# Two interleaved layers of sliding-window attention and gated linear units: the transposes moved off the DMA queue

## The chip, the cores and the metric

The kernel runs on one core of a Trainium2 chip. The metric is device time in microseconds (us) of the whole launch; lower is better. The time before is a median of three runs. One more execution was taken with the hardware profiler, and all rows shown come from that one.

## The reference

Two kinds of layer, A and B, alternate twice over x of 2048 tokens and 512 features in bf16:

```
x = x + A(layernorm(x));  x = x + B(layernorm(x))      # and both once more
A: qkv = x @ wqkv;  32 heads of 16;  scores = q k^T / 4
   masked to 0 <= query - key < 256;  p = softmax(scores);  (p v) @ wo
B: (sigmoid(x @ w_gate) * (x @ w_up)) @ w_down          # 512 -> 1792 -> 512
```

The weights are the same in both rounds. The layer norm has no learned scale or shift.

## The kernel before

**Tiles and stages.** x stays on chip as 16 tiles of 128 tokens by 512 features (`xsb`). Each of the two rounds (L = 0, 1) does the same for every tile t:

- *Norm* (`layer_norm`, L629): mean and variance on VectorE (L649, L651), the inverse root on GpSimd (L662, L663), the normed tile `xn` on VectorE (L681). This happens twice per tile and round, ahead of the attention (key "p") and ahead of the GLU (key "g"), so 64 times. TensorE contracts over partitions, so `xn` must be turned into `xnT`. Ten tiles are turned by TensorE: four transposes of 128 by 128 into a PSUM bank (L704) and one copy to SBUF on ScalarE or VectorE (L738, L740). They are the first eight of the first attention and the GLU tiles 0 and 1 of the first round (`alone`, from OPT g1 and `turn`). The other 54 go in pairs through 27 DMA transposes on the SP queue (L728).
- *Projections*: q and k feature-major in groups of four tiles (L780, L811), v token-major (L847), each copied out of PSUM by ScalarE or VectorE. k is split in two masked halves (L826). V carries a column of ones per head, so that the values' matmul also yields the softmax's sum; two shifted copies of it are made by plain DMAs (L1388).
- *Scores and values*: a tile's scores are worked off in five visits (two for the last tile), 154 in all. A visit fills four PSUM banks (`Sps`; L1106, L1117, L1127), ScalarE takes the exponential (L1159), VectorE multiplies the masks in (L1037). Then `values` (L1161, matmul L1186) makes the outputs of 16 heads in one bank: four heads side by side in a column block, each head on 32 partitions (16 outputs, the sum, padding).
- *Attention output* (`after_values`, L1192): the bank is copied out to `OTs` (L738 or L740), a DMA transpose turns it token-major into `Oq` (L1205), VectorE takes the reciprocal of the sums (L1240) and multiplies (L1241) into `On`, and a second DMA transpose turns that into `OnT` (L1213), which the output projection reads (L970). L976 adds the result to x. For the first two tiles of round 0 both turns are made by TensorE instead (`turn_by_pe`, L1253; the norm reads PSUM).
- *GLU* (`glu_units`): gate and up matmuls (L875) on 1, 2 or 4 tiles at once, so 128, 256 or 512 columns; tanh on ScalarE (L893), product on VectorE (L901); `down_units` (L939), and L948 adds to x. The list GLU says which tiles go together.

**Order.** Nothing is ordered by the hardware alone: `Plan` is a small planner that runs when the kernel is built. It keeps a clock, one queue per engine with a priority per kind of task, and assumed costs in ns; each engine's instruction stream is what it picks. `pick` chooses TensorE's next step: a visit of scores no earlier than `pace` after the last one, the values when their masks are done, else a dense unit by rank. Dense units and values share four PSUM banks; a unit's bank is free when its copy is done. DMAs carry an assumed issue cost and slack. The priorities, slacks, ranks and paces stand in SEGMENTS, a table that may change them at every fifth visit. `keep_warm` (L1370) issues idle matmuls before the first weights land. Rings limit how far work runs ahead: 2 `xn` (pairs), 3 `xnT`, 1 `OTs`, 1 `Oq`, 1 `On`, 2 `OnT`.

Of the kernel before, what the change touches and what calls it, by code (L numbers as in the profile page):

```python
# [9 lines left out]
ALU = mybir.AluOpType  # L10
BF16 = mybir.dt.bfloat16
F32 = mybir.dt.float32
P = 128
# [43 lines left out]
def pool_ns(n):  # L57
# [5 lines left out]
GLU = [[[1, 1, 1, 1, 2, 2], [1, 1, 1, 1, 2, 2], [1, 1, 2, 2, 2], [1, 1, 1, 1, 1, 1, 1, 1], [2, 2, 2, 2], [1, 1, 2, 1, 1, 2], [2, 2, 4]], [[4, 4, 4, 2, 2], [4, 4, 4, 2, 2], [4, 4, 2, 2, 4]]]  # L63
# [6 lines left out]
ARRIVE = dict(x0=3280, x1=4280, x2=5600, k=8560, q=10000, v=10900)  # L70
# [3 lines left out]
RATE = ((10900, 40.0), (1e9, 345.0))  # L74
# [3 lines left out]
LINE_NS = 3550  # L78
# [3 lines left out]
OPT = dict(gu='SP', g1=1, bk=3, bq=2, wide=0, r0=2, g0=5, g2=0, x0=1, eps=1, hold=1, own=1, ck=0, cq=2, turn=2,  # L82
    split=0, mo=0, at=3, r1=1, near=1)
RANK = dict(x3=31008.59915082838, wd=1355.5443193096523)


class Late(dict):


    def __missing__(self, name):  # L90
        return {"vv": self["v"], "tp": 0, "tp_g": 2}[name] if name in ("vv", "tp", "tp_g") else self[name[:-1]]


SEGMENTS = {
    0: (False, dict(st_x0=16.387, ap_x0=6.225, xt_x0=7.482, st_x1=3.545, ap_x1=7.915, xt_x1=12.783, st_x=12.637,
        ap_x=12.681, xt_x=-4.829, st_p=-0.616, ap_p=7.606, xt_p=5.184, st_g=-0.445, ap_g=2.621, xt_g=-2.868,
        st_g0=3.679, ap_g0=-17.463, xt_g0=-4.767, tp=8.093, tp_g=6.212, q=-2.808, q0=10.418, q1=-21.607, k=-11.975,
        k0=12.49, k1=0.894, s=-4.824, s0=2.968, s1=4.16, v=-0.758, v0=18.344, v1=21.96, vv=-1.006, exp=-7.486,
        exp0=-1.374, m0=3.414, m00=5.808, e0=-7.871, e00=2.35, e1=1.881, e10=8.977, m2=1.191, m20=5.467, th=14.916,
        mu=-10.778, dn=-19.706, add=-0.599, add0=7.919, out=-15.994, mv=30.614, mv0=7.196, oq=-9.099, oq0=-8.293,  # L100
        no=9.304, no0=-3.84, on=10.221, on0=-11.559, vc=9.867, vc0=-2.298), dict(xt=3835, oq=509, on=2499, vc=2407),
        dict(tp=-26.503, o=-3.164, lead=15.979, far=73.841, v=2.438, g=58.124, d=37.228, feed=44.486,
        x3=31008.59915082838, wd=1355.5443193096523, go=147.94192547482436), 1500.53),
    5: (False, {}, {}, {}, 1500.53),
    10: (False, {}, {}, {}, 1500.53),
    15: (False, {}, {}, {}, 1500.53),
    16: (False, {}, {}, {}, 1690.96),
    20: (False, {}, {}, {}, 1690.96),
    25: (False, {}, {}, {}, 1690.96),
    26: (True, dict(st_p=1.672, ap_p=36.822, xt_p=-2.918, st_x=-11.841, ap_x=0.6, xt_x=14.582, st_g=-13.947,  # L110
        ap_g=-7.573, xt_g=7.949, q=-14.515, k=21.982, s=1.709, v=-1.564, exp=-39.767, m0=2.485, e0=7.8, e1=8.391,
        m2=14.841, th=1.045, mu=-20.576, dn=-2.4, add=-13.535, out=27.454, mv=35.926, oq=-4.313, no=8.505, on=12.109,
        vc=-17.889), dict(xt=240, oq=3128, on=2754, vc=10020), dict(tp=36.947, o=-40.166, lead=9.199, far=17.491,
        v=-2.507, g=13.193, d=13.247, feed=-46.58, go=607.5028023985727), 2727.3),
    30: (False, dict(ap_x=1.293, dn=-2.072), dict(oq=2609), dict(feed=-47.788), 2681.58),
    35: (False, dict(st_p=0.51, ap_g=-7.3, mu=-24.39), dict(oq=2664, on=2941), dict(o=-39.26, lead=12.63, go=494),
        2681.58),
    40: (False, dict(st_p=1.672, ap_g=-7.573, mu=-20.576), dict(xt=779, oq=2609, on=2754), dict(o=-40.166,
        lead=9.199, go=607.5028023985727), 2620.7),
    45: (False, dict(st_p=0.82), dict(xt=240), dict(g=8.75, go=213), 1879.3),  # L120
    50: (False, dict(st_p=1.672), {}, dict(g=13.193, go=607.5028023985727), 2681.58),
    55: (False, {}, dict(xt=86), dict(lead=13.76), 2574.1),
    60: (False, {}, dict(xt=240), dict(lead=9.199), 2681.58),
    65: (False, {}, {}, {}, 2681.58),
    70: (False, {}, {}, {}, 2764.0),
    75: (False, {}, {}, {}, 2681.58),
    80: (False, {}, {}, {}, 2717.8),
    85: (False, dict(k=22.27, e0=8.47), {}, dict(far=18.98, v=-3.32, g=13.07), 2632.8),
    90: (False, dict(q=-15.93, k=21.982, e0=7.8, e1=11.21, add=-11.69), dict(on=2458), dict(lead=9.39, far=17.491,
        v=-2.507, g=14.8), 2717.8),  # L130
    95: (False, dict(q=-14.515, e1=8.391, add=-13.535), dict(on=2754), dict(lead=9.199, g=13.193), 2717.8),
    100: (False, {}, {}, {}, 2717.8),
    105: (False, {}, {}, {}, 2717.8),
    110: (False, {}, {}, {}, 2717.8),
    115: (False, {}, {}, dict(go=877), 2868.0),
    120: (False, {}, {}, dict(go=607.5028023985727), 2717.8),
    125: (False, {}, {}, {}, 2717.8),
    130: (False, {}, {}, {}, 2717.8),
    135: (False, {}, dict(oq=2597), dict(lead=8.49, far=16.64), 2717.8),
    140: (False, {}, dict(oq=2609), dict(lead=9.199, far=17.491), 2717.8),  # L140
    145: (False, {}, {}, {}, 2717.8),
    150: (False, {}, {}, {}, 2717.8),
}


def segments():

    out, now = {}, [Late(), {}, {}, 0]
    for slot, (new, prio, slack, rank, pace) in SEGMENTS.items():
        now = [Late(prio) if new else Late({**now[0], **prio}), {**now[1], **slack}, {**now[2], **rank}, pace]  # L150
        out[slot] = now
    return out
# [263 lines left out]
class Net:  # L416


    def __init__(self, ctx, tc, A_x, wqkv, wo, w_gate, w_up, w_down, out):
# [44 lines left out]
        ring("xn", 2, [P, 2, D])  # L464
# [4 lines left out]
        ring("On", 1, [P, 8, 4, 16])  # L469
# [159 lines left out]
    def layer_norm(self, key, t, deps):  # L629

        nc, pl = self.nc, self.pl
        alone = key[:2] == ("p", 0) and t < NBG * (1 + OPT["g1"]) or key[0] == "g" and self.by_pe(key[1], t)
        done = self.xn_ready[key, t]
        if alone:
            box, tiles = {"i": 0}, [t]
        else:
            box = self.pairs.setdefault((key, t // 2), {"i": t % 2, "ready": []})
            tiles = [t // 2 * 2, t // 2 * 2 + 1]
        mine = 0 if alone else t % 2
# [5 lines left out]
        def stats(e):  # L645
            if "st" not in box:
                box["st"] = self.take("st")
            st = box["st"][0][:, mine]
            nc.vector.bn_stats(out=st[:, 0:6], in_=self.xsb[:, t, :])  # L649
            if not first:  # L650
                nc.vector.bn_aggr(out=st[:, 6:8], in_=st[:, 0:6])  # L651

        def moments(e):
            st = box["st"][0][:, mine]
            nc.vector.bn_aggr(out=st[:, 6:8], in_=st[:, 0:6])
            nc.vector.tensor_scalar(out=st[:, 9:10], in0=st[:, 7:8], scalar1=1e-5, scalar2=None, op0=ALU.add)

        def root(e):
            st = box["st"][0]
            n = len(tiles)  # L660
            if not first:
                nc.gpsimd.tensor_scalar(out=st[:, 0:n, 9:10], in0=st[:, 0:n, 7:8], scalar1=1e-5, scalar2=None, op0=ALU.add)  # L662
            nc.gpsimd.tensor_tensor(out=st[:, 0:n, 8:9], in0=st[:, 0:n, 9:10], in1=self.nhalf[:, 0:n].rearrange("p (n x) -> p n x", x=1),  # L663
                                    op=ALU.pow)
# [10 lines left out]
        def apply(e):  # L675
            box["xn"] = b = self.take("xn")
            if key not in self.xnT:
                self.xnT[key] = self.take("xnT")
            for k, tt in enumerate(tiles):
                st = box["st"][0][:, k]  # L680
                nc.vector.tensor_scalar(out=b[0][:, k, :], in0=self.xsb[:, tt, :], scalar1=st[:, 6:7], scalar2=st[:, 8:9],  # L681
                                        op0=ALU.subtract, op1=ALU.mult)
# [6 lines left out]
        if not alone:  # L689
            box["ready"].append(a.done)  # L690
            if len(box["ready"]) < 2:
                return
        b = pl.task({"POOL": 800 - 230 * first}, root, box.get("ready", [a.done]), self.prio["st_" + kind])
        self.roots[key + (t,)] = b.done
        c = pl.task({"DVE": 60 + 346 * len(tiles)}, apply, [b.done], self.prio["ap_" + kind], can, port=True)
# [3 lines left out]
        i = tiles[0] % NBG  # L699
        if alone:  # L700
            def steps(bank):
                pt = self.tp_view(bank)
                xn = box["xn"][0][:, 0]
                return [(57, lambda c=c: nc.tensor.transpose(pt[:, c, :], xn[:, c * P:(c + 1) * P], self.ident[:]))  # L704
                        for c in range(KT)]

            def evac(u):
                pt = self.tp_view(u.bank)
                if key == ("p", 0, 0) and t < OPT["split"]:
                    half, both = KT // 2, Event()  # L710
# [9 lines left out]
            def ready():  # L720
                u = Unit(("tp", t), steps, [], False, evac)
                if key == ("p", 0, 0) and OPT["own"]:
                    u.own = BANKS + t
# [873 lines left out]
```

## Time and profile before

| what | us |
|---|---|
| median of three runs | 540.66 (540.53 to 541.17) |
| the profiled execution | 540.86 |
| its span, first to last instruction | 539.1 |
| busy: TensorE / VectorE / ScalarE / GpSimd | 524.0 / 417.1 / 384.8 / 43.6 |
| exponentials (L1159), 154 | 283.0 |
| GLU matmuls (L875), 1456 recorded | 256.5 |

In the profile's rows PE is TensorE's matmuls, PEld its weight loads (they overlap), DVE VectorE, ACT ScalarE, POOL GpSimd, and SPq the queue from which SyncE issues DMAs. L with a number is a line of the kernel. A group's row gives line, engine, operation, out<-in, shape and count; then busy us and mean ns of one; then the idle time of the engine just before them. A row of the timeline gives start and duration in us. A matmul's duration contains its way through the array, so several that follow each other overlap; their distance in time is what they cost. The granted TensorE clock was full in all 40 slices. Some matmul records are missing from a trace.

The 87 DMA transposes appear in the list of DMA issues with these median times from issue to landing: Oq<-OTs x30 3.3 us, OnT<-On x30 2.5 us, xnT<-xn x27 3.6 us.

### The profile page before, as it was taken

The page shows a single profiled execution, that of the slowest core. Times are in us where ns is not written, and L with a number is a line of the kernel's source. Part 1 is how long each engine was busy: PE and PEld are TensorE (multiplying, and loading weights), DVE is VectorE, ACT ScalarE, POOL GpSimd, SP SyncE. Part 2 cuts the span into 40 slices and gives each one's busy share as a digit, 9 for nine tenths or more (in the row PEclk, how much of TensorE's full clock was granted, in tenths as well). Part 3 has the DMA queues.
Part 4 walks back from the last instruction along what each step waited for, and adds up shares of the span by engine and source line. Part 5 has one row for each costly group of instructions (what it writes and reads, how often), then busy time and mean ns, then how long its engine had stood idle before and what let it go on. Part 6 is the DMA issues. An engine that isn't in the chain of part 4 may idle for free.

```text
span 539.1 us, 21310 instructions
## 1 busy us (share of the span) xinstructions
PE 524.0 (97%) x9606; PEld 293.1 (54%) x9674; DVE 417.1 (77%) x841; ACT 384.8 (71%) x384; POOL 43.6 (8%) x99
## 2 busy tenths in 40 slices
PE   8999999999999999999999999999999999999997
PEld 8446845758657544544444445444444454445873
DVE  6999989898798897779896989789787774442442
ACT  4999988979889797789688887688877751230330
POOL 4401100000001010000110100100000000000000
PEclk9999999999999999999999999999999999999999
DMA  8851533234223326225235323332143234101001
GB/s 259 320 149 52 82 82 52 53 71 74 39 56 42 72 41 93 50 56 72 47 51 72 52 54 45 68 61 62 33 80 52 51 43 75 34 1 39 2 11 39
DMA packets 95083, 36.23 MB, mean 67 GB/s; under 512 B 78352, under 2 KB 93968, under 8 KB 94992
## 3 DMA queue, kind: packets, MB, share of 16 engines
q1 hardware_dynamic: 93872, 33.82, 31.9%
q8 instruction: 75, 1.23, 1.0%
q10 hardware_dynamic: 1120, 1.05, 0.7%
q14 instruction: 16, 0.13, 0.1%
HBM read 9.70 MB, written 2.10 MB: 22 GB/s over the span
## 4 chain that ended last, share of the span: by engine, by line
PE 90%; ACT 4%; DVE 2%; issue 2%; DMA 1%; DVEq 0%
PE bank L875 36%; PE bank L939 18%; PE bank L1186 9%; PE Sps L1106 7%; PE bank L970 5%; PE bank L811 5%; PE bank L780 4%; PE bank L847 4%; PE Sps L1117 2%; ACT PTring L1159 2%; ACT edge L1159 1%; DMA xnT<-xn 1%; DMA xsb<-in_A_x_dram 0%; ACT qT L738 0%; DVE st L649 0%
## 5 line engine op out<-in xcount | busy, mean ns | idle before, releaser
L1159 ACT ACTIVATE PTring<-Sps 128x2048 bf16<-128x2048 f32 (+1 forms) x122 | 226.3, 1855 | 44.5 <-PE Sps L1106 41.0
L875 PE MATMUL bank<-xnT,wu 128*128 128x512 bf16 (+2 forms) x728 | 128.7, 297 | 0.5 <-issue 0.5
L875 PE MATMUL bank<-xnT,wg 128*128 128x512 bf16 (+2 forms) x728 | 127.8, 298 | 0.2 <-issue 0.2
L893 ACT ACTIVATE hT<-bank 128x256 bf16<-128x256 f32 (+1 forms) x154 | 71.5, 483 | 68.1 <-PE bank L875 67.5
L901 DVE SCALAR_TENSOR_TENSOR hT<-hT,bank 128x256 bf16<-128x256 bf16 (+1 forms) x154 | 80.6, 537 | 50.9 <-ACT hT L893 26.3
L939 PE MATMUL bank<-wd,hT 128*128 128x512 bf16 (+2 forms) x429 | 101.8, 372 | 3.2 <-issue 2.4
L875 PEld LDWEIGHTS <-wg 128*128 128x128 bf16 x728 | 61.2, 98 | 37.4 <-issue 2.7
L875 PEld LDWEIGHTS <-wu 128*128 128x128 bf16 x728 | 61.8, 98 | 35.3 <-issue 2.6
L939 PEld LDWEIGHTS <-hT 128*128 128x128 bf16 x462 | 42.5, 98 | 47.0 <-issue 1.9
L1159 ACT ACTIVATE edge<-Sps 128x2048 bf16<-128x2048 f32 (+1 forms) x32 | 56.7, 1773 | 13.4 <-PE Sps L1117 13.1
L1186 PE MATMUL bank<-PTring,Vaug 128*32 128x64 bf16 (+1 forms) x2880 | 51.8, 203 | 0.7 <-issue 0.7
L1186 PEld LDWEIGHTS <-Vaug 128*32 128x32 bf16 x2880 | 43.9, 97 | 12.3 <-issue 10.6
L1037 DVE TENSOR_TENSOR PTring<-PTring,mask 128x1024 bf16<-128x1024 bf16 x64 | 43.6, 683 | 7.9 <-ACT PTring L1159 7.7
L1106 PE MATMUL Sps<-qT,kTp 32*128 32x256 bf16 (+3 forms) x1216 | 47.4, 248 | 0.9 <-ACT edge L1159 0.4
L740 DVE CAST OTs<-bank 128x512 bf16<-128x512 f32 x52 | 37.8, 728 | 13.4 <-PE bank L1186 13.2
L649 DVE BATCH_NORM_STATS2 st<-xsb 128x6 f32<-128x512 bf16 x64 | 43.9, 686 | 1.7 <-DMA xsb<-in_A_x_dram 1.1
L662 POOL TENSOR_SCALAR st<-st 128x2 f32<-128x2 f32 (+1 forms) x33 | 11.3, 342 | 411.2 <-DVE st L651 411.2
L1186 PE MATMUL bank<-edge,Vl 128*32 128x64 bf16 x1024 | 44.6, 193 | 0.0
L1106 PEld LDWEIGHTS <-kTp 32*128 32x128 bf16 x1216 | 17.8, 92 | 43.1 <-issue 41.4
L1037 DVE TENSOR_TENSOR edge<-edge,maske 128x1024 bf16<-128x1024 bf16 x60 | 39.8, 680 | 1.8 <-ACT edge L1159 1.5
L1186 PE MATMUL bank<-edge,Vh 128*32 128x64 bf16 x896 | 40.6, 193 | 0.0
L1037 DVE TENSOR_TENSOR PTring<-PTring,maskn 128x1024 bf16<-128x1024 bf16 x56 | 38.2, 682 | 1.8 <-ACT PTring L1159 1.8
(75 smaller groups left out, 524.0 us busy)
## 6 DMA issues: line engine op xcount, KB each, us to landing
Vl<-Vaug SPq DMA_DIRECT2D x32, 68.0 KB, 2.4
out_dram<-xsb SPq DMA_DIRECT2D x15, 128.0 KB, 2.1
Vh<-Vaug SPq DMA_DIRECT2D x28, 68.0 KB, 2.2
wg<-in_B_w_gate_dram SPq DMA_DIRECT2D x2, 896.0 KB, 9.4
wu<-in_B_w_up_dram SPq DMA_DIRECT2D x2, 896.0 KB, 13.8
wd<-in_B_w_down_dram SPq DMA_DIRECT2D x7, 256.0 KB, 3.3
xsb<-in_A_x_dram SPq DMA_DIRECT2D x6, 256.0 KB, 6.7
wq<-in_A_wqkv_dram ACTq DMA_DIRECT2D x3, 256.0 KB, 5.5
```

The lines of the kernel that those rows point to most:

```text
L649: nc.vector.bn_stats(out=st[:, 0:6], in_=self.xsb[:, t, :])
L740: self.nc.vector.tensor_copy(out=out, in_=in_)
L811: return [(mm_ns(w), lambda kt=kt, o=o: nc.tensor.matmul(self.banks[bank][:, o:o + w], lhsT=self.wq[:, kt, D + cq * P:D + cq * P + P], rhs ...
L875: return [(mm_ns(w), lambda i=i, j=j, fc=fc, wt=wt, kt=kt: self.nc.tensor.matmul(pt[:, i, j, :], lhsT=wt[:, kt, fc * P:(fc + 1) * P], rhs= ...
L893: self.nc.scalar.activation(out=self.hT[:, ch[0] * GW:ch[0] * GW + size], in_=pt, func=AF.Tanh, scale=0.5)
L901: self.nc.vector.scalar_tensor_tensor(out=h, in0=h, scalar=1.0, in1=pt, op0=ALU.add, op1=ALU.mult)
L939: nc.tensor.matmul(self.banks[bank][:, 0:w], lhsT=self.hT[:, at:at + P], rhs=self.wd[:, fc, d], start=fc == 0, stop=fc == FC - 1)
L970: return [(mm_ns(D), lambda c=c: nc.tensor.matmul(self.banks[bank][:], lhsT=b[0][:, c, :], rhs=self.wot[:, c, :], start=c == 0, stop=c == ...
L1037: done = pl.task({"DVE": dve_bf_ns(1024)}, lambda e: nc.vector.tensor_tensor(out=r, in0=r, in1=m.to_broadcast([P, 16, HP]), op=ALU.mult), ...
L1106: nc.tensor.matmul(self.sps[:, m, o:o + n * HP], lhsT=kTp[32 * m:32 * m + 32, i, tt, e, :], rhs=self.qT[32 * m:32 * m + 32, i, q0:q0 + n * ...
L1159: nc.scalar.activation(out=out, in_=src, func=AF.Exp, scale=scale)
L1186: nc.tensor.matmul(o, lhsT=Va[:, c0:c0 + 32], rhs=p(h), start=k == 0 or t == 0, stop=k == len(parts) - 1 or t == 0, tile_position=(0, 32 * g))
```

## The change

It takes every DMA transpose out.

- All 64 normed tiles take the way over TensorE: four transposes into a PSUM bank and one copy. Tiles are normed one by one, not in pairs; the ring `xn` becomes four single tiles.
- The attention outputs are turned by VectorE's own transpose, which turns blocks of 32 by 32 in place of the whole. The first turn takes the 1024 columns of `OTs`, the second the 512 of `On`. The way over TensorE for the first two tiles goes.
- For this the heads are dealt out otherwise: in `values`, column block and 32-partition group are assigned so that after the two block turns the features stand where the output projection's weights expect them. The norm becomes one reciprocal and two products of half the size.
- SEGMENTS goes; the planner has one set of priorities, slacks and ranks for the first 22 visits and one for the rest, and paces in PACE. Its assumed arrival times are a little different. In GLU, round 0 takes its first eight tiles one by one (before: 1, 1, 2, 1, 1, 2), and round 1 takes four groups of four (before: 4, 4, 4, 2, 2).

The core of the diff:

```diff
-GLU = [[[1, 1, 1, 1, 2, 2], [1, 1, 1, 1, 2, 2], [1, 1, 2, 2, 2], [1, 1, 1, 1, 1, 1, 1, 1], [2, 2, 2, 2], [1, 1, 2, 1, 1, 2], [2, 2, 4]], [[4, 4, 4, 2, 2], [4, 4, 4, 2, 2], [4, 4, 2, 2, 4]]]
+GLU = [[[1, 1, 1, 1, 2, 2], [1, 1, 1, 1, 2, 2], [1, 1, 2, 2, 2], [1, 1, 1, 1, 1, 1, 1, 1], [2, 2, 2, 2], [1, 1, 1, 1, 1, 1, 1, 1], [2, 2, 4]], [[4, 4, 4, 4], [4, 4, 4, 2, 1, 1], [4, 4, 2, 1, 1, 4]]]
+PACE = [2681.81, 1328.37, 1196.7, 872.42, 21.95]
...
-        ring("xn", 2, [P, 2, D])
+        ring("xn", 4, [P, 1, D])
-        ring("On", 1, [P, 8, 4, 16])
+        ring("On", 1, [P, 4, 4, 2, 16])
...
     def layer_norm(self, key, t, deps):
-        alone = key[:2] == ("p", 0) and t < NBG * (1 + OPT["g1"]) or key[0] == "g" and self.by_pe(key[1], t)
...
-            d = pl.dma(1240, 262144, lambda: nc.sync.dma_start_transpose(
-                out=self.xnT[key][0][:, i:i + 2].rearrange("p t c q -> p (t c) q"),
...
+        def steps(bank):
+            pt = self.tp_view(bank)
+            xn = box["xn"][0][:, 0]
+            return [(57, lambda c=c: nc.tensor.transpose(pt[:, c, :], xn[:, c * P:(c + 1) * P], self.ident[:]))
+                    for c in range(KT)]
...
+            d = pl.task({"ACT": act_ns(KT * P), "DVE": dve_ns(KT * P) + 100}, lambda e: self.copy(
+                e, self.xnT[key][0][:, i], pt), [u.done], self.prio["tp" if key[0] == "p" else "tp_g"])
...
     def values(self, L, t, half, bank):
-            heads = range(16 * half + 4 * col, 16 * half + 4 * col + 4)
+            heads = [16 * half + 8 * (col // 2) + 2 * g + col % 2 for g in range(4)]
...
     def after_values(self, L, t, half, bank, done):
-        def turn():
+        def turn(e):
             box["Oq"] = self.take("Oq")
-            nc.sync.dma_start_transpose(out=box["Oq"][0][:], in_=box["OTs"][0][:].rearrange("p c q -> p (c q)"))
+            nc.vector.transpose(out=box["Oq"][0][:].rearrange("p c q -> p (c q)"), in_=box["OTs"][0][:].rearrange("p c q -> p (c q)"))
 
         def norm(e):
             box["Rt"], box["On"] = self.take("Rt"), self.take("On")
-            self.normalize(box["Oq"][0][:], box["Rt"][0], box["On"][0])
+            Oq, Rt, On = box["Oq"][0], box["Rt"][0], box["On"][0]
+            tv = Oq[:].rearrange("p c (b r) -> p c b r", r=32)
+            nc.vector.reciprocal(out=Rt[:], in_=tv[:, :, :, 16:17])
+            for e in range(2):
+                nc.vector.tensor_tensor(out=On[:, :, :, e, :], in0=tv[:, e:8:2, :, 0:16],
+                                        in1=Rt[:, e:8:2].to_broadcast([P, 4, 4, 16]), op=ALU.mult)
...
-        if self.by_pe(L, t):
-            self.turn_by_pe(L, t, box)
-            return
-        b = pl.dma(1250, 262144, turn, [box[0], box[1]], self.prio["oq0" if early else "oq"], base=1950, slack=self.slack["oq"])
+        b = pl.task({"DVE": 1130}, turn, [box[0], box[1]], self.prio["oq0" if early else "oq"], lambda: self.has("Oq"), port=True)
...
-        d = pl.dma(1240, 131072, turn2, [c.done], self.prio["on0" if early else "on"], slack=self.slack["on"])
+        d = pl.task({"DVE": 600}, turn2, [c.done], self.prio["on0" if early else "on"], lambda: self.has("OnT"), port=True)
...
     def pace(self, s):
-        return self.tables[3] if s < len(self.visits) else 0
+        if s >= len(self.visits):
+            return 0
+        if s < PACE[4]:
+            return PACE[2 if s < EARLY else 3]
+        return PACE[self.visits[s][0]]
```

## The prediction, made before the changed kernel was run

> **What bounds the kernel now.** I read the page's rows of busy time and of the slices first, for the engine that is always on:
>
> ```profile
> span 539.1 us, 21310 instructions
> PE 524.0 (97%) x9606; PEld 293.1 (54%) x9674; DVE 417.1 (77%) x841; ACT 384.8 (71%) x384; POOL 43.6 (8%) x99
> ...
> PE   8999999999999999999999999999999999999997
> ...
> DVE  6999989898798897779896989789787774442442
> ACT  4999988979889797789688887688877751230330
> ```
>
> TensorE is full in every slice; VectorE and ScalarE are nearly full for 32 slices (430 us), then under half. A busy TensorE may hide waits, so I read the timeline around 300 us next, for what one step really takes:
>
> ```profile
> 300.84 0.38 PE L875 MATMUL bank<-xnT,wu 128*128 128x512 bf16 x1
> ...
> 301.15 0.40 PE L1106 MATMUL Sps<-qT,kTp 32*128 32x256 bf16 x8
> ...
> 301.48 1.90 PE L847 MATMUL bank<-wq,xnT 128*128 128x512 bf16 x8
> ...
> 304.29 0.27 PE L1186 MATMUL bank<-PTring,Vaug 128*32 128x128 bf16 x8
> ...
> 305.10 1.04 PE L875 MATMUL bank<-xnT,wg 128*128 128x512 bf16 x4
> ```
>
> Eight matmuls of 512 columns take 1.90 us, one alone 0.38: they follow each other at (1.90 - 0.38)/7 = 0.217 us, call it 0.216. The matmul started at 300.84 is streamed by 301.06 and dense work resumes at 301.48: a visit of scores costs 0.43 us, switching included. The values of a half tile hold TensorE from 304.29 to 305.10, 0.81 us.
>
> Now the sum. Dense work in units of 512 columns, from the code: GLU 896, down 448, q, k and v 384, output projection 128, together 1856 x 0.216 = 400.9 us. Visits 154 x 0.43 = 66.2. Values 64 x 0.81 = 51.8. Transposes 64 x 0.056 (below) = 3.6. Before the first projection (8.8 us, the first start of the k matmuls in the answer on tile xnT) and behind the last matmul (535.8 to 539.1) 12.1; outside the span 540.86 - 539.1 = 1.8. Total 536.4 of the profiled execution's own 540.86: **some 4 us of waiting in the whole kernel**. A change can gain little by removing waits; whatever it gives TensorE to do is paid in full.
>
> **TensorE's part of the change.** Removed: 27 DMA transposes of pairs of normed tiles (L728), and the 24 transposes of attention outputs (L1253). Added: the path of L704 for all 64 normed tiles instead of 10, so 54 x 4 = 216 transposes; net 192. Their price is in the timeline of TensorE near 54 us:
>
> ```profile
> 54.18 0.39 PE L704 MATMUL bank<-ident,xn 128*128 128x128 bf16 x4
> 54.40 0.55 PE L875 MATMUL bank<-xnT,wu 128*128 128x128 bf16 x7
> ```
>
> Four transposes start at 54.18, the next matmul at 54.40: 0.055 to 0.056 us each. So 192 x 0.056 = **+10.8 us**, on the engine that sets the end. The Trainium skill speaks harder against this: "TensorE: Matmul & The Clock Gate", section "Back-to-back issue gap", gives about 81 ns for a sustained pair of weight load and 128-column matmul, which would make 15.6 us; its "Part 4: PE-mode transpose" reports about 275 ns in a kernel, which would make 53 us. The second is a duration, like the 219 ns of the row on L704, and durations overlap here. I take the row's pitch, and keep 15.6 as the upper end.
>
> The GLU's new grouping replaces 448 matmuls of 256 columns by 448 of 128 and 112 of 512. By pitches from the same timelines (0.056, 0.109, 0.216): 25.1 + 24.2 - 48.8 = **+0.5 us**. More columns at once in the last group takes nothing from the tail, where TensorE already streams without a gap.
>
> **What the DMA transposes cost today.** The list of waits has one line of TensorE for them:
>
> ```profile
> PE bank L780 <- DMA xnT<-xn: 1.0, 1, 1.0
> ```
>
> Removing it and its 0.5 us in the weight load gives back **about 1 us**; SP's 87 transposes of some 1.25 us leave the SP queue, and the copies of V behind them start earlier, but no wait of TensorE names those copies. If they mattered unseen, the gain is bounded by the 4 us of all waiting.
>
> **VectorE and ScalarE.** The nearest rows, in the groups by form:
>
> ```profile
> L681 DVE TENSOR_SCALAR xn<-xsb,st 128x512 bf16<-128x512 bf16 x64 | 23.7, 406 | 2.9 <-POOL st L663 2.7
> L1241 DVE TENSOR_TENSOR On<-Oq,Rt 128x512 bf16<-128x512 bf16 x30 | 20.7, 692 | 1.0
> L1240 DVE RECIPROCAL Rt<-Oq 128x32 f32<-128x32 bf16 x30 | 10.3, 343 | 0.0
> L738 ACT COPY xnT<-bank 128x512 bf16<-128x512 bf16 x2 | 1.4, 685 | 0.0
> L740 DVE COPY xnT<-bank 128x512 bf16<-128x512 bf16 x4 | 1.6, 412 | 0.0
> ```
>
> No row shows a 32-by-32 transpose. L1241 takes 0.692 us for 512 elements; with the masks' 0.683 for 1024 (L1037) as the fast end, 1024 elements lie between 0.68 and, at two cycles an element, 2.3 us. "Vector Engine (DVE) Microarchitecture Reference", section 3.8, says that the array sustains one element per cycle per lane; L1241 is the row of that rate (0.16 us fixed and 0.53 for 512), so I take 0.16 + 1.07 = 1.23 us for the first turn and 0.69 for the second, estimates: 32 x 1.92 = **61 us on VectorE** (36 to 112). The planner's own figures in the diff, 1130 and 600 ns, are close. The norm becomes one reciprocal and two products of 256 (0.692 - 0.267 = 0.425 us each): 32 x 1.19 = 38.2 for 33.1, +5. Copies of 54 transposed tiles: half on VectorE at 0.41 (+11), half on ScalarE at 0.63 (+17). The GLU's grouping and the two lost OnT copies give back 3 and 2.5. So VectorE has about 417 + 74 = 491 us, ScalarE 385 + 15 = 400; GpSimd's roots one by one add some 22 us to an engine that is 8% busy.
>
> Is that covered? By stage, from the table of windows:
>
> ```profile
> 30.00:60.00 30.00, 29.39 (x678) 19.61 (x678) 28.71 (x65) 28.52 (x29) 5.55 (x10) 1.00 0.36 92
> ...
> 430.00:460.00 30.00, 29.75 (x493) 14.78 (x494) 18.44 (x33) 10.55 (x14) 0.93 (x2) 1.00 0.34 55
> 460.00:500.00 40.00, 39.79 (x199) 19.65 (x202) 15.50 (x26) 9.51 (x17) 0.93 (x2) 1.00 0.08 23
> 500.00:540.00 40.00, 35.62 (x272) 26.22 (x273) 14.21 (x32) 9.61 (x25) 0.00 (x0) 1.00 0.06 18
> ```
>
> (after the length: TensorE, weight loads, VectorE, ScalarE.) Less the last three stages, VectorE has 369.0 and ScalarE 355.1 us in the first 430: 84% of the two. With nearly all the 89 us added there, 813 of 2 x 441 is 92%. The window of 30 to 60 us shows both at 95% with TensorE at 98%, so 92% fits, if casts move to ScalarE (most OTs casts are on VectorE today, 52 of 64, and may run on either). But that same window has no room left: its four or so tiles bring 12 us more, 6 to each engine; GLU matmuls are there to fill in, so I take **+2 us** of 0 to 6.
>
> The new waits: each group of transposes needs one of four banks until its copy is done, and TensorE is in order, so behind a late copy or a late xn stand all scores and dense work. On VectorE a turn of 1.23 us stands ahead of GLU products and casts that free banks. For 54 groups between nothing and 0.2 us each (0 to 11) I take **+2 us**, since the ten groups of today (answer on L704) waited 2.1 us for xn, in four waits.
>
> Sum on the profiled execution: 540.86 + 10.8 + 0.5 - 1.0 + 2 + 2 = 555.2; the median lies 0.2 lower, **555.0 us**.
>
> **The rivals.** *TensorE as above*, 548 to 562: chance 0.67. *VectorE becomes the bound of the attention stage*: if turns cost two cycles an element (+52 us), the two engines need 865 us; at the 95% that the trace shows as reachable this is 455 us instead of 441, so 555 + 14 = 569. For it: the saturated early window, and that turns can't move to ScalarE. Against: section 3.8, the planner's figures, and the tail, to which GLU work can move. Chance 0.25, 562 to 580. *Not slower*: the transposes fall into dead time. A visit's 0.43 us holds about 0.21 of streaming, so 154 visits hold 33 us that do nothing; a group of four (0.22 us) placed there would be free, and 540.7 + 0.5 - 1 = 540.2 results. It decides once a group costs under 0.02 us of its own. Against it: the dead time is switching, at both ends of a visit, and more dense work beside it doesn't shorten it (in the timeline scores start 0.09 us behind a full stream). Chance 0.08, mostly through a cheaper start and fewer switches together.
>
> **How the numbers follow.** About 0.2% is what a measurement of this kernel tells from no change. Slower 0.92, within 0.2% 0.04, faster 0.04, all of the last two from the third case. The range runs from 547 (waits of nothing, 10.8 alone, and less) to 569 (the second case's middle, which also covers 15.6 for the transposes).
>
> **What would show it.** After: 256 transposes of xn with a pitch of 0.056 us, no DMA transposes, TensorE still full in all slices; VectorE near 490 us; turns near 1.23 and 0.69 us. Idle TensorE in the first 60 us, or scores that start late behind VectorE, speak for the second case. A span under 545 would mean that switching or the start got cheaper, and that my sum counts waits as work.

## The result, and the profile after

| | us | |
|---|---|---|
| before, median of three | 540.66 | 540.53 to 541.17 |
| after, median of three | 566.36 | 565.68 to 566.81 |
| ratio | 1.0471 | 1.0448 to 1.0495 (95%) |

The change makes the kernel 25.7 us slower. The profiled execution took 566.81 us, its span 565.1. The page of the changed kernel, the rows shown of before:

```profile
span 565.1 us, 22076 instructions
PE 548.7 (97%) x9998; PEld 300.0 (53%) x9998; DVE 461.9 (82%) x921; ACT 407.8 (72%) x424; POOL 61.4 (11%) x153
...
PE   8999899999999999999999999999999999999997
...
DVE  6999999999988899996699986989768999852332
ACT  3999989979999887891699827999189985530330
...
PE 66%; DVE 21%; ACT 5%; issue 4%; DMA 2%; ACTq 1%; POOL 0%; SPq 0%; DVEq 0%
```

TensorE is as full as before by this measure. Its 548.7 us can't be set against the 524.0 of before, whose trace lacks matmul records (9606 beside 9674 weight loads): before_retuned, a run below with the same work and a full trace, has 530.2. The last row is the one that speaks: it gives the chain that ended last, by engine. Before, the same row read `PE 90%; ACT 4%; DVE 2%`; now a fifth of the chain runs over VectorE. A busy row can't show that, because a matmul of 512 columns lasts 0.38 us and the next may start 0.216 us after it, so that its duration covers short waits behind it.

The new operations, in the groups by form (busy us and mean ns behind the bar):

```profile
L1138 DVE STREAM_TRANSPOSE Oq<-OTs 128x1024 bf16<-128x1024 bf16 x32 | 39.7, 1240 | 1.6 <-ACT OTs L676 1.0
L1151 DVE STREAM_TRANSPOSE OnT<-On 128x512 bf16<-128x512 bf16 x32 | 22.6, 706 | 0.0
L1146 DVE TENSOR_TENSOR On<-Oq,Rt 128x256 bf16<-128x256 bf16 x64 | 24.4, 422 | 1.1
L676 ACT COPY xnT<-bank 128x512 bf16<-128x512 bf16 x36 | 20.1, 603 | 46.4 <-PE bank L647 46.4
L678 DVE COPY xnT<-bank 128x512 bf16<-128x512 bf16 x24 | 9.3, 415 | 0.4 <-PE bank L647 0.3
L647 PE MATMUL bank<-ident,xn 128*128 128x128 bf16 x240 | 19.7, 219 | 2.2 <-DVE Vaug L678 1.2 <-DVE xn L629 0.3
```

The turns last 1.24 and 0.71 us, as estimated. The wait of TensorE's matmuls for a DMA transpose is gone. Its list of waits, without the lines put down to "issue", now begins:

```profile
PEld L903 <- DVE OnT L1151: 4.8, 11, 0.7
PEld L647 <- DVE xn L629: 3.4, 7, 1.3
PE Sps L1039 <- ACT PTring L1092: 1.9, 4, 0.8
PE Sps L1039 <- ACT edge L1092: 1.5, 3, 0.6
PE bank L647 <- DVE Vaug L678: 1.2, 4, 0.6
```

Eleven output projections wait for the second turn, seven groups of transposes for the normed tile; these two are waits of weight loads (PEld), which overlap the matmuls ahead of them in part. The last line's kind is seen in the timeline, first VectorE's part of it and then TensorE's:

```profile
92.06 0.35 DVE L1144 RECIPROCAL Rt<-Oq 128x32 f32<-128x32 bf16 x1
92.44 0.76 DVE L1146 TENSOR_TENSOR On<-Oq,Rt 128x256 bf16<-128x256 bf16 x2
93.11 0.74 DVE L759 TENSOR_SCALAR kTp<-kTp,rm 128x512 bf16<-128x512 bf16 x2
93.77 1.28 DVE L678 CAST Vaug<-bank 128x512 bf16<-128x512 f32 x2
```
```profile
93.26 0.61 PE L647 MATMUL bank<-ident,xn 128*128 128x128 bf16 x8
94.50 0.33 PE L647 MATMUL bank<-ident,xn 128*128 128x128 bf16 x3 [0.64 <-DVE Vaug L678]
94.77 0.40 PE L1039 MATMUL Sps<-qT,kTp 32*128 32x64 bf16 x16
```

Two groups of transposes went through; the third needs a bank that holds V, whose cast stands behind the norm and the masks of k in VectorE's queue. TensorE stops, and the scores behind it with it.

By stage, in the table of windows (TensorE, weight loads, VectorE, ScalarE):

```profile
30.00:60.00 30.00, 26.78 (x578) 16.78 (x580) 29.55 (x66) 28.97 (x34) 5.82 (x14) 1.00 0.27 87
...
460.00:500.00 40.00, 39.82 (x749) 19.41 (x747) 35.46 (x66) 21.77 (x22) 3.31 (x8) 1.00 0.05 16
500.00:540.00 40.00, 39.06 (x188) 17.90 (x187) 13.82 (x21) 10.04 (x17) 0.00 (x0) 1.00 0.04 14
```

Between 30 and 60 us TensorE is busy 2.6 us less than before, with VectorE and ScalarE at 98 and 97%. Attention goes on into the second row (the last exponential starts at 483.6 us, before at 437.8), so less dense work is left for the end than before.

**How much is waiting.** From the starts of the matmuls one can sum what a start lies behind the one before plus its stream (0.216 us for 512 columns and so on), less the usual cost of a change between dense work, scores and values (the median of each kind, 0.09 to 0.17 us). Within dense work and at those changes this gives **17 us** after. Before, where records are missing, it can't be had cleanly; two runs below that are nearly the kernel before and whose trace is complete (before_retuned, h_before_no_masks) give **5 us** each. So beside these two some 12 us are new waits; 5 of them lie in the first 100 us. TensorE's stream has 11.7 more: 192 transposes x 0.056 = 10.8, the GLU's grouping 0.5, eight idle matmuls more in the first 60 us (88 of L1257 for 80) 0.4. Two smaller terms come from the same starts: the first projection begins 1.1 us later than in before_retuned (9.8 for 8.7 us), and inside the values, some of which wait for their masks, the starts lie 3.2 us further apart in total. Together that is 28.0 us, and the span is 28.2 us longer than that of before_retuned. The kernel before is itself 2.2 us longer than before_retuned, so its own waits may be nearer 7 than 5, and the new ones nearer 10 than 12.

### The profile page after: what moved, and what is told of

Read it like the earlier page. It is cut to its first block, busy times and chain, and to the rows that moved or that the text cites. A ratio compares the mean times of both kernels' runs of the same rounds, so it can differ in the third digit from the quotient of the medians.

```text
span 565.1 us, 22076 instructions
## 1 busy us (share of the span) xinstructions
PE 548.7 (97%) x9998; PEld 300.0 (53%) x9998; DVE 461.9 (82%) x921; ACT 407.8 (72%) x424; POOL 61.4 (11%) x153
## 4 chain that ended last, share of the span: by engine, by line
PE 66%; DVE 21%; ACT 5%; issue 4%; DMA 2%; ACTq 1%; POOL 0%; SPq 0%; DVEq 0%
PE bank L808 29%; PE bank L872 14%; PE bank L1119 6%; PE Sps L1039 5%; PE bank L903 5%; DVE PTring L970 3%; DVE kTp L759 3%; PE bank L713 2%; DVE Oq L1138 2%; PE bank L780 2%; DVE edge L970 2%; ACT PTring L1092 2%; DVE On L1146 2%; DVE st L600 1%; DMA wg<-in_B_w_gate_dram 1%
## 5 line engine op out<-in xcount | busy, mean ns | idle before, releaser
L1092 ACT ACTIVATE PTring<-Sps 128x2048 bf16<-128x2048 f32 (+1 forms) x122 | 226.7, 1859 | 29.2 <-PE Sps L1039 26.6
L808 PE MATMUL bank<-xnT,wg 128*128 128x128 bf16 (+1 forms) x784 | 125.7, 288 | 1.3 <-ACT xnT L676 0.9
L808 PE MATMUL bank<-xnT,wu 128*128 128x128 bf16 (+1 forms) x784 | 125.6, 288 | 0.0
L834 DVE SCALAR_TENSOR_TENSOR hT<-hT,bank 128x512 bf16<-128x512 bf16 (+1 forms) x140 | 78.0, 570 | 27.0 <-PE bank L808 23.1
L826 ACT ACTIVATE hT<-bank 128x512 bf16<-128x512 f32 (+1 forms) x140 | 69.3, 518 | 33.3 <-PE bank L808 33.1
L808 PEld LDWEIGHTS <-wg 128*128 128x128 bf16 x784 | 58.9, 98 | 40.4 <-issue 4.0
L808 PEld LDWEIGHTS <-wu 128*128 128x128 bf16 x784 | 59.1, 98 | 38.3 <-issue 2.3
L612 POOL TENSOR_SCALAR st<-st 128x1 f32<-128x1 f32 x60 | 17.8, 297 | 426.1 <-DVE st L602 426.0
L676 ACT COPY xnT<-bank 128x512 bf16<-128x512 bf16 x36 | 20.1, 603 | 46.4 <-PE bank L647 46.4
L881 DVE SCALAR_TENSOR_TENSOR xsb<-bank,xsb 128x512 bf16<-128x512 f32 (+2 forms) x33 | 22.0, 665 | 28.1 <-PE bank L872 28.0
L1138 DVE STREAM_TRANSPOSE Oq<-OTs 128x1024 bf16<-128x1024 bf16 x32 | 39.7, 1240 | 1.6 <-ACT OTs L676 1.0
```

The source lines that it names most:

```text
L808: return [(mm_ns(w), lambda i=i, j=j, fc=fc, wt=wt, kt=kt: self.nc.tensor.matmul(pt[:, i, j, :], lhsT=wt[:, kt, fc * P:(fc + 1) * P], rhs= ...
L826: self.nc.scalar.activation(out=self.hT[:, ch[0] * GW:ch[0] * GW + size], in_=pt, func=AF.Tanh, scale=0.5)
L834: self.nc.vector.scalar_tensor_tensor(out=h, in0=h, scalar=1.0, in1=pt, op0=ALU.add, op1=ALU.mult)
L881: e = pl.task({"DVE": dve_ns(w)}, lambda e: nc.vector.scalar_tensor_tensor(out=self.xsb[:, t, d], in0=self.banks[u.bank][:, 0:w], scalar=0 ...
L1092: nc.scalar.activation(out=out, in_=src, func=AF.Exp, scale=scale)
L1138: nc.vector.transpose(out=box["Oq"][0][:].rearrange("p c q -> p (c q)"), in_=box["OTs"][0][:].rearrange("p c q -> p (c q)"))
```

## The experiments

My theory: TensorE pays the stream of every added transpose, and the rest is TensorE waiting behind VectorE. The rivals: the transposes cost nothing beside other waits; the loss is one of order, since each engine's order is written out by the planner and its tables were replaced too.

### One part at a time, under the tables of before

**x only (a_x_pe).** The kernel before with:

```diff
-        alone = key[:2] == ("p", 0) and t < NBG * (1 + OPT["g1"]) or key[0] == "g" and self.by_pe(key[1], t)
+        alone = True
-        ring("xn", 2, [P, 2, D])
+        ring("xn", 4, [P, 1, D])
```

> The kernel before with one part of the change: all 64 normed tiles turned by TensorE, singly, everything else (DMA turns of the attention outputs, TensorE turns for the first two tiles, tables) as before. Theory 'TensorE pays stream time': 216 transposes x 0.056 us = 12.1 us on a full engine, so 551 to 555 us. Theory 'the planner's tables carry the loss': the tables are those of before, so little over 540.7 plus 12. Theory 'transposes stall TensorE through banks and copies': 558 or more.

Measured: 579.14 us (ratio 1.0714, 1.0698 to 1.0730).

**Turns only (b_turns_dve).** The kernel before with the changed `after_values`, the heads dealt anew and `On` in its new shape:

```diff
-            heads = range(16 * half + 4 * col, 16 * half + 4 * col + 4)
+            heads = [16 * half + 8 * (col // 2) + 2 * g + col % 2 for g in range(4)]
...
-        b = pl.dma(1250, 262144, turn, [box[0], box[1]], self.prio["oq0" if early else "oq"], base=1950, slack=self.slack["oq"])
+        b = pl.task({"DVE": 1130}, turn, [box[0], box[1]], self.prio["oq0" if early else "oq"], lambda: self.has("Oq"), port=True)
```

> The kernel before with the other part: attention outputs turned and normed on VectorE with the heads dealt anew, for all tiles; normed x as before (27 DMA transposes). TensorE loses the 24 transposes of the first two tiles (-1.3 us), VectorE gains some 66 us. Theory 'TensorE pays stream time': 539 to 543 us. Theory 'VectorE pays': its queue holds up banks and masks, 548 us or more, idle TensorE mostly in the first 100 us.

Measured: 554.93 us (1.0264, 1.0246 to 1.0281).

**Both (c_both_old_tables)**: the two edits above together.

> Both parts of the change under the tables of before (SEGMENTS, GLU grouping, arrival times). If the changed kernel's loss lies in its tables, this is clearly below 566, some 553 to 556. If it lies in the transposes, the turns and what they hold up, it is near 566 or above, since these tables were not made for it.

Measured: 596.41 us (1.1033, 1.1015 to 1.1051).

**New tables, old transposes (d_new_tables_dma).** The changed kernel with the `layer_norm`, `after_values`, head order and rings of before, and `g1=1`, so that eight first tiles go over TensorE as before. It also has the diff's option `bq` (2 to 3: one more q unit of the first group is made tile by tile, with the same stream).

> The changed kernel's tables (PRIO, PACE, GLU grouping, arrival times) with all transposes of before (27 + 60 DMA transposes). Theory 'TensorE pays stream time, and VectorE its queue': 541 to 545 us. Theory 'the tables carry the loss': 550 us or more, as the changed kernel less the 11 us of its transposes.

Measured: 567.31 us (1.0497, 1.0481 to 1.0514).

My theory missed wherever it gave a range (a, b and d), and the branches that allow for stalls hold only because they were open upwards. That of b_turns_dve also put the idle mostly into the first 100 us: TensorE was busy 4.0 us less than before there (92.2 for 96.2), and 4.0 less again between 100 and 300. Each part alone costs far more than its work, both together cost 30 us more than the changed kernel, and the new tables cost 26.6 us where nothing else is new. Part of this is TensorE's clock: the traces have stretches at half of it, 20.5 us in c and in d, 10.2 in a and 3.4 in b. Work takes at most twice as long there (eight transposes 1.03 us in a, for 0.61 in a row below), so they cost at most half their length. The rest I put down to order: a part that is taken over under tables made for another kernel can't be priced. In d_new_tables_dma this can be seen with the eye, in the table of windows (TensorE, weight loads, VectorE, ScalarE, GpSimd; then TensorE's granted clock):

```profile
440.00:450.00 10.00, 9.79 (x146) 4.30 (x146) 8.58 (x18) 8.85 (x7) 0.00 (x0) 1.00 0.27 43
...
460.00:465.00 5.00, 1.98 (x128) 1.52 (x121) 3.55 (x8) 4.25 (x3) 0.00 (x0) 0.77 0.14 30
465.00:470.00 5.00, 2.46 (x112) 1.75 (x100) 2.17 (x4) 3.75 (x2) 0.00 (x0) 0.50 0.29 56
...
475.00:480.00 5.00, 2.18 (x97) 1.51 (x93) 2.92 (x6) 3.89 (x5) 0.71 (x2) 0.50 0.51 57
```

From 452.5 to 482.6 us TensorE has only scores, values and a dozen dense matmuls; the scores wait for exponentials, with half a clock on top for 20 us. The GLU's matmuls lie ahead of this stretch and behind it. I read that as dense work spent too early. The next two groups therefore hold the order fixed, or choose it anew for each kernel.

### The order held fixed

In these four the planner isn't told of the edit, so that all else is issued in the same order.

**Each transpose twice (e_twice_transposed)**, in the changed kernel:

```diff
-            return [(57, lambda c=c: nc.tensor.transpose(pt[:, c, :], xn[:, c * P:(c + 1) * P], self.ident[:]))
+            return [(57, lambda c=c: [nc.tensor.transpose(pt[:, c, :], xn[:, c * P:(c + 1) * P], self.ident[:]) for _ in range(2)])
                     for c in range(KT)]
```

> The changed kernel with every transpose of a normed tile issued twice (same input, same output), and the plan not told of it, so that the order of all else stays. 256 more transposes x 0.056 us = 14.3 us of TensorE's stream. Theory 'TensorE pays the stream time of each transpose': 578 to 582 us. Theory 'the transposes fall into dead time beside visits and waits': under 571.

Measured: 572.97 us (1.0603, 1.0587 to 1.0619), so 6.6 us more than the changed kernel. A row of its timeline:

```profile
142.20 0.61 PE L647 MATMUL bank<-ident,xn 128*128 128x128 bf16 x8
```

Eight in 0.61 us, one lasts 0.219: (0.61 - 0.219)/7 = 0.056 us each, no discount for repeating. The stream did grow by 14.3 us, but the waits by the sum above fell from 17 to 11. My reading, not tested further: time given to TensorE is time in which VectorE and ScalarE catch up. Both expectations missed, in an instructive way: the changed kernel is bound by TensorE and by its waits in turn, and added stream was paid by half here.

**More matmuls before (g_before_more_matmuls)**: in the kernel before, the first matmul of each v unit and output projection is issued twice.

```diff
-                start=kt == 0, stop=kt == KT - 1)) for kt in range(KT)]
+                start=kt == 0, stop=kt == KT - 1 or more == 1) for more in ((1, 0) if kt == 0 else (0,))]) for kt in range(KT)]
```

> The kernel before with 64 more matmuls of 512 columns: the first matmul of each v unit and of each output projection is issued twice, the plan not told. 64 x 0.216 = 13.8 us of TensorE's stream, and nothing for any other engine. Theory 'TensorE has no slack, whatever it is given is paid': 553 to 556 us. Theory 'there is slack in the plan': under 549.

Measured: 556.24 us (1.0292, 1.0277 to 1.0308), 15.7 us for 13.8 of stream: a little over what was expected. Its trace has 3.4 us at half a clock (458.2 to 461.7 us), which is up to 1.7 us; the one execution with the full clock throughout took 555.59. In the kernel before there is no slack, and what TensorE gets is paid in full.

**No masks, after and before (h_after_no_masks, h_before_no_masks)**: the mask tasks stay in the plan but issue nothing.

```diff
-            done = pl.task({"DVE": dve_bf_ns(1024)}, lambda e: nc.vector.tensor_tensor(
-                out=r, in0=r, in1=m.to_broadcast([P, 16, HP]), op=ALU.mult), [x.done, self.has_mask],
+            done = pl.task({"DVE": dve_bf_ns(1024)}, lambda e: None, [x.done, self.has_mask],
```

> The changed kernel without the mask multiplications (180 instructions, some 121 us of VectorE; the scores are left unmasked), the plan not told, so that the order of all else stays. Theory 'some 14 of the 26 us are TensorE waiting behind VectorE's longer queue': 554 to 559 us. Theory 'the waits are for exponentials, banks on ScalarE and the start': 563 or more.

> The kernel before without the mask multiplications (the scores are left unmasked), the plan not told. By both theories TensorE hardly waits for VectorE here: 537 to 540 us. Its distance to the changed kernel without masks is then what TensorE itself has more to do, 12 to 16 us.

Measured: 561.73 us after (1.0396, 1.0379 to 1.0413) and 538.93 before (0.9969, 0.9958 to 0.9979). So the changed kernel gains 4.6 us and the kernel before 1.6; the first lies between the two expectations, the second in its range, but their distance, expected at 12 to 16 us, is 22.8. VectorE's 121 us less hardly touch the changed kernel's 17 us of waits: by the same sum 16 are left. What falls is the time inside the values, by 3.7 us, and the first projection starts at 8.9 us. The chain of the changed kernel without masks:

```profile
PE 76%; ACT 12%; issue 5%; DVE 4%; DMA 2%; ACTq 1%; SPq 0%
```

VectorE fell from 21% to 4% of the chain, and ScalarE took its place with 12%. My theory that the waits are VectorE's load fell here. An order that asks for the next scores when an exponential is due, with too little dense work at hand, would fit, since TensorE would then wait for whoever is last; this run alone doesn't show it, and the next group tests the order.

### The order chosen anew

Now only numbers are changed: priorities, slacks, ranks and paces, chosen by a random search for a shorter plan, for each kernel anew. Nothing that is computed changes, only the order and, for a few copies and casts, the engine. How far each search went is not on record, so a part of the differences may be its luck. Two of many such lines, from the changed kernel and from the kernel before:

```diff
-PACE = [2681.81, 1328.37, 1196.7, 872.42, 21.95]
+PACE = [2699.177, 818.589, 1931.906, 2581.572, 25.318]
...
-    50: (False, dict(st_p=1.672), {}, dict(g=13.193, go=607.5028023985727), 2681.58),
+    50: (False, dict(st_p=4.086), dict(), dict(g=29.567, go=0), 1951.506),
```

**The changed kernel (after_retuned).**

> The changed kernel with only the numbers of its tables (PRIO, LATE_PRIO, SLACK, RANK, PACE and their like) chosen anew by a random search for a shorter plan; transposes, turns, head order and GLU grouping untouched. Theory 'about half of the waits come from an order that doesn't suit, not from the engines' work': 556 to 561 us. Theory 'VectorE's and ScalarE's longer queues must cost this much': 564 or more. TensorE's own 12 us stay in any case, so not under 552.

Measured: 557.77 us (1.0331, 1.0309 to 1.0352).

**Turns only (turns_on_dve_retuned).**

> The kernel before with the attention outputs' turns on VectorE, normed x by DMA (as in b_turns_dve), and the numbers in SEGMENTS chosen anew by the same kind of search. Theory 'the 14 us of b_turns_dve are an order made for another kernel': 540 to 546 us, since TensorE even loses 1.3 us of work and VectorE stays under 90%. Theory 'the VectorE turns themselves cost': 551 or more.

Measured: 543.00 us (1.0043, 1.0030 to 1.0056).

**x only (x_pe_retuned).**

> The kernel before with all normed tiles turned by TensorE, attention outputs by DMA (as in a_x_pe), and the numbers in SEGMENTS chosen anew by the same kind of search. TensorE's 12.1 us cannot be ordered away: 553 to 561 us. Theory 'transposes fall into dead time once the order suits': under 548.

Measured: 556.22 us (1.0287, 1.0273 to 1.0301).

**The kernel before (before_retuned), the control.**

> Control: the kernel before, the numbers in SEGMENTS chosen anew by the same kind of search. If the search helps any kernel, this falls clearly below 540; if the tables of before already suit it, 538 to 543 us.

Measured: 538.64 us (0.9962, 0.9949 to 0.9974).

The first three lie where the first theory of each put them; the control lies where its two ranges overlap, with a small gain. The price of the parts is now plainer: turning on VectorE costs 2.2 us beside the kernel before, turning x on TensorE 15.4, both 17.0; beside the control, which was tuned by the same means, 4.4, 17.6 and 19.1. The search gave the changed kernel 8.6 us and the kernel before 2.2, so some 6 us of the 25.7 were an order that suited the changed kernel less well than the old one suited the old. The chains of the three, in this order (changed kernel, turns only, x only):

```profile
PE 77%; DVE 13%; ACT 5%; issue 2%; DMA 1%; POOL 1%; DVEq 0%; ACTq 0%
```
```profile
PE 71%; DVE 22%; ACT 3%; issue 1%; DMA 1%; POOL 1%; SPq 0%; ACTq 0%
```
```profile
PE 86%; DVE 7%; ACT 4%; POOL 2%; issue 1%; DMA 0%; ACTq 0%
```

With the turns on VectorE alone the chain runs over VectorE as much as in the changed kernel under its own tables (22% for 21%), and the time is still within 0.5% of before: a chain that touches an engine is not yet a wait. By the sum of waits the three have 12, 10 and 10 us, where before_retuned has 5. With the stream (+11.7, -1.3, +12.1) and 5 taken off, this makes +18.7, +3.7 and +17.1 beside the control, against 19.1, 4.4 and 17.6 measured. TensorE's transposes are the loss that none of these orders takes away.

before_retuned is also the version that beats both kernels: 0.4% faster than the kernel before, with none of the change in it.

## Why the prediction was right, and where its sizes were off

The time lay inside the range (547 to 569), 11 us above the likeliest value, and the direction was right for the reason given, TensorE's transposes. That 566 lies inside is in part luck: the main case reached only to 562, and the range went up to 569 for the sake of the rival with VectorE as the bound, whose 562 to 580 holds the measured time.

- *TensorE's transposes, +10.8*: right. The pitch of 0.056 us held in 256 and in 512 transposes (e_twice_transposed); the 81 ns that the Trainium skill's "TensorE: Matmul & The Clock Gate" gives in "Back-to-back issue gap" were not seen. "Whatever it gives TensorE to do is paid in full" holds for the kernel before (15.7 for 13.8), and no longer for the changed one (6.6 for 14.3).
- *GLU grouping +0.5, gone DMA waits -1*: too small to be told apart; idle matmuls added 0.4 that I hadn't counted.
- *VectorE's operations*: 1.24 and 0.71 us for the two turns against my 1.23 and 0.69. The rate that I took for one element per cycle was the right choice between 0.68 and 2.3. VectorE's sum was not right: 461.9 us for my 491. Casts of OTs, V and k that went to ScalarE are 15 us of this (OTs casts on VectorE 40 of 64, before 52), fewer copies of xn than half 3 (24 of 64), and some 11 are more instructions that overlap the one ahead of them in the trace and so count once.
- *Waits, +2 at the start and +2 for banks*: this is the step that was mis-sized: 10 to 12 us instead of 4 (with the 1 us given back, 3 net), and some 4 more at the first projection and inside the values, for which the sum had no term. I read from the old trace that ten groups of transposes had waited little and that 92% of two engines fits where 95% had been reached, and priced the new tasks under that order. But an order is made for its tasks: the replaced tables were a part of the change that I had in the diff and put at nothing. Other numbers in them are worth 8.6 us on the changed kernel, and d_new_tables_dma shows that an order that doesn't suit costs over 25. Of the start I took 2 us, and the window from 30 to 60 us alone lost 2.6.
- *The rival with VectorE as the bound* (569) gave nearly the measured time for a wrong reason: two cycles an element are refuted (1.24 us for the 2.3 they would take), no engine but TensorE was full, and taking 121 us from VectorE gave back only 4.6 us. The signs that I had named for it did show, TensorE less busy before 60 us and scores behind VectorE's queue (at 93.9 us), so they don't tell this case from the first.
- *The rival in which transposes fall into dead time* is refuted for the kernel before: x_pe_retuned costs 15.4 us for 12.1 of stream. In the changed kernel something like it happens, at waits that the change itself made.

What stays open: the last 5 to 7 us of waits over the kernel before in after_retuned, and how much of the 6 us of order is the search. The planner's short figures for the turns (1130 and 600 for 1240 and 706 ns) would make output projections come too early, and eleven of them do wait for OnT, but a plan with the measured figures wasn't tried.

## What to carry to other kernels

If one engine is full with hardly a wait in its stream, work moved onto it is paid in full, however short each piece is, and a transfer that nobody waits for is free where it is: move transposes away from DMA only if a wait on the full engine names them. Work moved between engines that have room (here 62 us of turns on VectorE at 84% busy) can be nearly free, if the order is made anew for it. Where an order is planned by tuned numbers, a part tried under numbers that were tuned for another kernel is not a measurement of that part: tune both sides by the same means, and the control too.

## What the runs showed of the hardware

The granted TensorE clock falls to a half while TensorE still works in bursts. In the windows of d_new_tables_dma above TensorE was busy for 6.4 of 10 us between 450 and 460 and for 2 of 5 after that, with no wait over 2.2 us in its list; from 462.7 to 483.2 us the clock was at 0.50. In a_x_pe one low stretch of 3.4 us was enough, and no wait of a matmul there is over 2.0 us (TensorE's busy time comes first, its clock behind GpSimd's):

```profile
322.30:325.70 3.40, 1.03 (x18) 0.40 (x16) 3.33 (x8) 3.03 (x3) 0.00 (x0) 1.00 0.00 0
325.80:329.20 3.40, 3.07 (x97) 2.41 (x99) 3.19 (x9) 3.26 (x4) 1.55 (x4) 0.50 0.02 5
```

In the changed kernel, whose waits are under 1.4 us and spread out, it stayed full. The Trainium skill ("TensorE: Matmul & The Clock Gate", section "HAM oscillation — how this bites in real kernels") names idle gaps over about 3.4 us as the danger; here a low share of work was enough, 1.0 of 3.4 us, with no gap so long. All stretches at half a clock between the first projection and the last matmul of these traces last 3.4, 6.8 or 20.5 us.

VectorE's transpose of 32-by-32 blocks in bf16 took 1240 ns for 1024 columns and 706 for 512: 534 ns for 512 more, which is 1.04 ns a column, with 0.17 us on top.
